# Both final masks of a pair by one minimum and one transposing DMA, in a top-k attention with a highway FFN

## The chip, the cores and the metric

The kernel runs on one core of one Trainium2 chip. Its time is the device time of one execution in microseconds (us); times here are medians of several runs on the same chip. Short names for the engines are those of the profile: PE is TensorE (PEld its weight loads), DVE is VectorE, ACT is ScalarE, POOL is GpSimd, SP is SyncE, whose work here is to issue DMAs.

## The reference

Eight batches of eight heads, 576 rows of 64 per head. Each row of scores keeps only its 32 largest; the others get no weight. The result, heads side by side, goes through a highway layer.

```
scores = scale * q @ k.T                              # 576 x 576 for each head
kth    = the 32nd largest score of each row
scores = where(scores >= kth, scores, -1e9)
attn   = exp(scores - max);  attn = attn / (sum(attn) + 1e-9)
x      = attn @ v, as 4608 x 512
H = relu(x @ w_h);  T = sigmoid(x @ w_t + b_t)
out = T * H + (1 - T) * x
```

## The kernel before, in words

A *unit* is up to 128 query rows of one head against all 576 keys; the last 64 rows of two heads share a unit. There are 288 units, taken two at a time as 144 *pairs*; a batch is 18 pairs. `step(i)` is one turn of a software pipeline over the pairs, and the order of the work on every engine is the order of the calls in `step`: no scheduler moves anything. In step i, pair i is in the middle of its threshold search, pair i+1 begins its own, pair i+2 gets its scores, pair i-1 gets its final mask, and pair i-3 is multiplied with V.

The threshold search of a pair runs as follows. TensorE computes the scores of both units into one tile of PSUM, `xs` (L309, L318; for the tail units L326, L335). VectorE takes the 8 largest of each sixth of a row, twelve instructions a pair (L353, `segments`). `refine` (L366 to L382) merges these into an estimate of the largest value and of a threshold, and writes both to `wall` with the reduction L382. ScalarE then counts with a sign function how many scores lie above the threshold (L397, `mask_count`) and writes a mask that TensorE adds to the scores in PSUM (L410), so that VectorE's next maximum (L420, `below`) finds the largest values below the threshold. From the count and these, L426, L436 (on GpSimd) and L439 pick the exact 32nd largest value. GpSimd multiplies out the biases for the exponential and the mask (L391, `biases`); an explicit dependency makes it wait for the second final mask of the step.

The final mask is made one step later. For the first unit of a pair ScalarE computes `r`, a huge number where the score is at or above the 32nd largest value and zero elsewhere (L443, `above`), and VectorE takes the minimum of the exponentials and `r` (L450, `keep_min`). For the second unit GpSimd computes `ro` as 1 or 0 (L454, `above_one`), and VectorE multiplies (L460, `keep_mul`). In 7 steps GpSimd has too much else, and VectorE makes the second mask in one instruction from the scores (L465, `keep`). Each masked unit goes to its own tile `ep` of 640 columns, 576 and 64 zeros, and SP issues a transposing DMA for each (L481) into a tile `et` of five 128 x 128 blocks. Two steps later TensorE multiplies these with V (L494). V carries a column of ones (L138), so that the sums of the exponentials come out as a 65th column.

Every four heads ScalarE copies the sums out of PSUM (L508, tile `xs` of the pool in SBUF, the same name as the scores' tile). TensorE's filler matmuls (L278, `spare`), which write to a fresh tile of the same PSUM bank, stand behind that copy. When a block of 128 rows has all its heads, its `norm` divides by the sums: VectorE adds 1e-9 and doubles (L557), takes the reciprocal (L559), and GpSimd multiplies in the next step (L564). A GpSimd DMA casts the block to `xb` (L582), SP transposes it to `xT` (L587), and the FFN's matmuls (L522, L532) follow in a later step. The tail of the kernel, `finish`, is written out by hand.

SP issues, in this order in a step: the transposes of the two masks, the transpose of `xb` where one is due, stores, and up to two loads of k and q.

In VectorE's order around the change, one step holds L366, L368, L426, L370, L373, L376, L439, L378, L450, L382, [L557,] L460, [L559,] then L353 of the next pair and L420.

Of the kernel before, what the change touches and what calls it, by code (L numbers as in the profile page):

```python
# [10 lines left out]
ALU = mybir.AluOpType  # L11
# [15 lines left out]
def kernel(  # L27
# [46 lines left out]
    gpool = ctx.enter_context(tc.tile_pool(name="g", bufs=2))  # L74
    epool = ctx.enter_context(tc.tile_pool(name="e", bufs=4))
    cpool = ctx.enter_context(tc.tile_pool(name="c", bufs=4))
    etpool = ctx.enter_context(tc.tile_pool(name="et", bufs=6))
    xpool = ctx.enter_context(tc.tile_pool(name="x", bufs=3))
# [28 lines left out]
    for i in range(NE):  # L107
        en = consts.tile([P, 2, 2, 16], FP32, name=f"en{i}")
        nc.vector.memset(en[:, 0, :, 0:1], 3.0e38)
        ends.append(en)  # L110
    csum = consts.tile([P, NU], FP32)
    nc.vector.memset(wall[:, 0:2, KTH : KTH + 1], 0.0)

    def kth(u):
        return wall[:, u + 2, KTH : KTH + 1]

    def tb(u):
        return be[:, u // 2, u % 2, 0:1]

    def eb(u):  # L120
        return be[:, u // 2 + 1, u % 2, 1:2]
# [14 lines left out]
    for i in range(2):  # L136
        vb = consts.tile([P, H, nck, DE], BF16, name=f"vb{i}")
        nc.gpsimd.memset(vb[:, :, :, D:DE], 1.0)  # L138
        vbs.append(vb)
    NEP = 4  # L140
    eps_sb = []
    for i in range(NEP):
        ep = consts.tile([P, SP], BF16, name=f"ep{i}")
        pad = S if i % 2 == 0 else 0
        nc.vector.memset(ep[:, pad : pad + SP - S], 0.0)
        eps_sb.append(ep)
# [266 lines left out]

    def expo(u, sc):
        e = epool.tile([P, S], BF16, name="e")
        nc.scalar.activation(e[:], sc, AF.Exp, bias=tb(u), scale=scale)  # L416
        return e

    def below(u, ps):
# [14 lines left out]
    def pick_a(pair, hit):  # L434
        u0, u1 = pair[0], pair[1] + 1
        nc.gpsimd.tensor_tensor(hit[:], hit[:], wall[:, u0:u1, THR:KTH], ALU.mult)  # L436
# [3 lines left out]

    def above(u, sc):
        r = epool.tile([P, S], BF16, name="r")
        nc.scalar.activation(r[:], sc, AF.Relu, bias=eb(u), scale=BIGK)  # L443
        return r


    def keep_min(u, e, r):
        ep = eps_sb[u % NEP]
        pad = (u % 2) * (SP - S)
        return ep, nc.vector.tensor_tensor(ep[:, pad : pad + S], e[:], r[:], ALU.min)  # L450

    def above_one(u, sc):
        r = epool.tile([P, S], BF16, name="ro")
        nc.gpsimd.tensor_scalar(r[:], sc, kth(u), None, ALU.is_ge)  # L454
        return r

    def keep_mul(u, e, r):
        ep = eps_sb[u % NEP]
        pad = (u % 2) * (SP - S)
        return ep, nc.vector.tensor_tensor(ep[:, pad : pad + S], e[:], r[:], ALU.mult)  # L460

    def keep(u, sc, e):
        ep = eps_sb[u % NEP]
        pad = (u % 2) * (SP - S)
        return ep, nc.vector.scalar_tensor_tensor(  # L465
            out=ep[:, pad : pad + S],
            in0=sc,
            scalar=kth(u),
            in1=e[:],
            op0=ALU.is_ge,  # L470
            op1=ALU.mult,
        )
# [5 lines left out]

    def transposes(ep):
        et = etpool.tile([P, nck, P], BF16, name="et")  # L480
        nc.sync.dma_start_transpose(et[:], ep[:])  # L481
        return et

# [65 lines left out]
    def ffn_pieces(b, qt, xs):  # L549
# [4 lines left out]
        def norm():  # L554
            xs3 = xs[:, 0 : nh * DE].rearrange("p (h e) -> p h e", e=DE)
            rinv = cpool.tile([P, H], FP32, name="rinv")
            nc.vector.tensor_scalar(rinv[:, 0:nh], xs3[:, :, D], 1e-9, 2.0, ALU.add, ALU.mult)  # L557
            yield
            nc.vector.reciprocal(rinv[:, 0:nh], rinv[:, 0:nh])  # L559
            x = xpool.tile([P, dm], FP32, name="x")  # L560
            st["x"] = x

            def scaled(e):
                e.tensor_tensor(  # L564
                    x[:, 0:w].rearrange("p (h d) -> p h d", h=nh),
                    xs3[:, :, 0:D],
                    rinv[:, 0:nh].unsqueeze(2).to_broadcast([P, nh, D]),
                    ALU.mult,
                )
                if by_dma:  # L570
                    casts.append(cast)
                else:
                    ready.extend([xt, hh, tt])

            pool_work.append((scaled, w))
            yield
# [63 lines left out]
    def blk_norm(k):  # L640
        nh, ng, w = shape_of(k["qt"])
        xs3 = k["xs"][:, 0 : nh * DE].rearrange("p (h e) -> p h e", e=DE)
        k["x"] = xpool.tile([P, dm], FP32, name="x")
        rinv = cpool.tile([P, H], FP32, name="rinv")
        nc.vector.tensor_scalar(rinv[:, 0:nh], xs3[:, :, D], 1e-9, 2.0, ALU.add, ALU.mult)
        nc.vector.reciprocal(rinv[:, 0:nh], rinv[:, 0:nh])
        nc.vector.tensor_tensor(
            k["x"][:, 0:w].rearrange("p (h d) -> p h d", h=nh),
            xs3[:, :, 0:D],
            rinv[:, 0:nh].unsqueeze(2).to_broadcast([P, nh, D]),  # L650
            ALU.mult,
        )
# [122 lines left out]
    def step(i):  # L775
# [25 lines left out]
        if prev:  # L801
            pu, ps_ = pairs[i - 1], st[i - 1]
            ps_["r"] = [above(pu[0], ps_["sc"][0])]
            ps_["r"].append(above_one(pu[1], ps_["sc"][1]) if len(pool_work) < (3 if last_steps else 5) else None)
        if late:
# [6 lines left out]
        ev = prep_filler() if to_prep and (i <= SPB or (len(to_prep) > 15 - k_in or len(layers) > 2) and i % 2) else None  # L812
        do_work(nc.gpsimd, 2 * dm if prev and ps_["r"][1] is None else dm)
        segs(i + 1, 2 * NSEG)
# [3 lines left out]
        if live:  # L818
            st[i]["e"] = [expo(pr[0], st[i]["sc"][0])]
        if nxt:  # L820
# [14 lines left out]
        if live:  # L835
            st[i]["e"].append(expo(pr[1], st[i]["sc"][1]))
            pass
        ra = refine(i + 1, st[i + 1]["cand"]) if nxt else iter(())

        def masked(s):  # L840
            if not prev:
                return None
            u = pu[s]
            if ps_["r"][s] is not None:
                ep, ins = (keep_min, keep_mul)[s](u, ps_["e"][s], ps_["r"][s])
            else:
                ep, ins = keep(u, ps_["sc"][s], ps_["e"][s])
            ps_["et"][s] = transposes(ep)
            return ins
# [3 lines left out]
        if live:  # L853
            hit = hits(pr)
            pick_a(pr, hit)
        added = bool(adds or casts)
        if adds:
# [11 lines left out]
        next(ra, None)  # L869
        masked(0)  # L870
        for _ in ra:
            pass
        scaling = norms.pop(0)() if norms else iter(())
        next(scaling, None)
        last = masked(1)
        if live:
            after(biases(i + 1), last)
        next(scaling, None)
        if nxt:
# [63 lines left out]
    def finish():  # L943
# [29 lines left out]
        while adds:  # L973
            do_add(i)
        relu = above(pu[0], old["sc"][0])
        zh = fps.tile([P, 512], FP32, tag="fp", name="fp")
        ep, last = masked(pu, 1, old)
        old["et"][1] = transposes(ep)
        if pool_work:
# [4 lines left out]
        below(pr[1], cur["ps"][1])  # L984
        es = [expo(u, cur["sc"][s]) for s, u in enumerate(pr)]
        cur["e"] = es
        x1 = xps.tile([P, 3 * BANK], FP32, tag="x", name="xs")
# [4 lines left out]

        hit = hits(pr)
        ep, _ = keep_min(pu[0], old["e"][0], relu)
        old["et"][0] = transposes(ep)
        nc.vector.tensor_tensor(hit[:], hit[:], wall[:, pr[0] : pr[1] + 1, THR:KTH], ALU.mult)
        pick_b(pr, hit)
        x2 = xps.tile([P, 3 * BANK], FP32, tag="x", name="xs")
        cur["et"] = [etpool.tile([P, nck, P], BF16, name="et") for s in range(2)]
        turned = None  # L1000
        for s, home in enumerate((bank(x2, 1), bank(x1, 0))):
            ep, last = masked(pr, s, cur)
            turned = home.bitcast(BF16)[:, 0:SP]
            for c in range(nck):
                nc.tensor.transpose(turned[:, c * P : (c + 1) * P], ep[:, c * P : (c + 1) * P], ident_b[:])
            nc.scalar.copy(cur["et"][s][:].rearrange("p c q -> p (c q)"), turned)
        sure(0, wall[:, 2 : NU + 2, KTH], 1.0)
# [40 lines left out]
    with tc.If(fine < 1):  # L1048
        with tc.For_i(0, B, 1) as bi:
# [26 lines left out]
            for pr in pairs[0 : NG // B]:  # L1076
                scs = copy_scores(scores(pr, prep)[2])
                ets = []
                for s, u in enumerate(pr):
# [13 lines left out]
                    nc.vector.tensor_scalar_mul(tb(u), w[:, 0:1], -scale)  # L1093
                    ep, _ = keep(u, sc, expo(u, sc))
                    ets.append(transposes(ep))
                pso = pso_tile()
# [42 lines left out]
```

## Time and profile before

| | us |
|---|---|
| median of 3 runs | 806.8 (805.77 to 807.28) |
| the profiled execution | 806.17 |
| its span, first to last instruction | 804.5 |
| VectorE busy | 772.8 |
| ScalarE busy | 757.2 |
| TensorE busy | 686.7 |
| GpSimd busy | 559.9 |

All sums below are made against the profiled execution. A row of the timeline has the start, the length, the engine, the line, the operation and its tiles (out<-in), how many instructions it merges, and in brackets how long the engine was idle before it and what ended that wait. A row of the groups has the total busy time and the mean of one in ns, then the idle time before them and its main cause. Rows of SP's queue (SPq) are the issuing of DMAs; the transfer itself lands later.

### The profile page before, as it was taken

How to read it: one execution, taken by the hardware profiler on the slowest of the kernel's cores; microseconds unless marked ns; L12 is line 12 of the kernel's file. 1: busy time of each engine (PE TensorE's matmuls, PEld its weight loads, DVE VectorE, ACT ScalarE, POOL GpSimd, SP SyncE). 2: the span in 40 equal slices, each digit the busy share in tenths (PEclk: the TensorE clock that was granted, in tenths of full speed). 3: DMA queues.
4: the chain of work that ended last, by engine and by line, in shares of the span. 5: the costliest groups of instructions: out<-in, count | busy, mean ns of one | idle time of the engine just before them, and what ended most of it. 6: DMA issues, size and time to landing. Idle time of an engine off the chain costs nothing.

```text
span 804.5 us, 20583 instructions
## 1 busy us (share of the span) xinstructions
PE 686.7 (85%) x6369; PEld 494.7 (61%) x6459; DVE 772.8 (96%) x4020; ACT 757.2 (94%) x1401; POOL 559.9 (70%) x712
## 2 busy tenths in 40 slices
PE   7889998888888888888987889888888888988884
PEld 5666766566666666566665666666666566665662
DVE  5999999999999999999999999999999999999996
ACT  5999999999999999999999999999999999999984
POOL 2666867777777767777767776777776777766750
PEclk9999999999999999999999999999999999999998
DMA  6789968996799667998669766898767996555653
GB/s 121 87 137 159 134 116 140 141 143 93 140 152 148 108 96 137 154 131 125 102 135 159 125 113 107 150 156 126 112 121 136 160 124 109 90 106 110 108 90 88
DMA packets 346359, 100.37 MB, mean 125 GB/s; under 512 B 330624, under 2 KB 338432, under 8 KB 346240
## 3 DMA queue, kind: packets, MB, share of 16 engines
q1 hardware_dynamic: 291024, 79.16, 54.1%
q0 software_dynamic: 53536, 19.34, 22.6%
q8 instruction: 53, 0.87, 0.4%
q10 hardware_dynamic: 1680, 0.46, 0.3%
q14 instruction: 66, 0.54, 0.2%
HBM read 31.72 MB, written 9.44 MB: 51 GB/s over the span
## 4 chain that ended last, share of the span: by engine, by line
ACT 37%; DVE 32%; PE 23%; DMA 4%; issue 3%; SPq 1%; another core or an unknown queue 0%; DVEq 0%; ACTq 0%
ACT m L397 15%; DVE wall L420 12%; DVE cand L353 9%; ACT e L416 7%; ACT sc L348 6%; PE pso L278 5%; ACT r L443 4%; PE xs L309 4%; PE xs L326 3%; DVE ep L450 3%; DMA xT<-xb 3%; PE fp L522 3%; PE xs L410 3%; PE pso L494 2%; ACT xs L508 2%
## 5 line engine op out<-in xcount | busy, mean ns | idle before, releaser
L353 DVE MAX8 cand<-xs 128x8 f32<-128x96 f32 x1728 | 297.5, 248 | 11.4 <-PE xs L335 6.2
L278 PE MATMUL pso<-cst,ident_b 128*128 128x252 bf16 x1841 | 246.8, 272 | 42.8 <-ACT xs L508 40.4
L454 POOL TENSOR_SCALAR ro<-sc,wall 128x576 bf16<-128x576 f32 x135 | 232.8, 1724 | 0.0
L416 ACT ACTIVATE e<-sc,be 128x576 bf16<-128x576 f32 x288 | 226.5, 787 | 0.1
L278 PEld LDWEIGHTS <-ident_b 128*128 128x128 bf16 x1841 | 173.4, 98 | 81.4 <-issue 49.5
L420 DVE MAX8 wall<-xs 128x8 f32<-128x576 f32 x288 | 204.3, 751 | 5.6 <-PE xs L410 3.5
L309 PE MATMUL xs<-kT,qT 64*128 64x256 f32 x1024 | 145.3, 400 | 30.6 <-DVE high L366 26.2
L348 ACT COPY sc<-xs 128x1152 f32<-128x1152 f32 x144 | 161.0, 1118 | 0.7 <-DVE cand L353 0.6
L309 PEld LDWEIGHTS xs<-kT,qT 64*128 64x128 f32 x1024 | 93.0, 186 | 61.3 <-issue 37.6
L397 ACT ACTIVATE m<-xs,wall 128x576 int8<-128x576 f32 x144 | 107.4, 746 | 18.2 <-DVE wall L382 17.1
L436 POOL TENSOR_TENSOR hit<-hit,wall 128x18 f32<-128x18 f32 x143 | 32.4, 227 | 121.2 <-DVE hit L426 114.0
L397 ACT ACTIVATE m<-sc,wall 128x576 int8<-128x576 f32 x144 | 111.4, 773 | 0.0
L443 ACT ACTIVATE r<-sc,be 128x576 bf16<-128x576 f32 x143 | 109.9, 769 | 0.0
L410 PE MATMUL xs<-m,ident_b 128*128 128x512 bf16 (+1 forms) x512 | 92.7, 274 | 17.3 <-ACT m L397 15.2
L494 PEld LDWEIGHTS <-et 128*128 128x128 bf16 (+1 forms) x1600 | 68.6, 100 | 19.2 <-issue 3.5
L391 POOL TENSOR_TENSOR be<-wall,fac 128x4 f32<-128x4 f32 x144 | 29.2, 203 | 72.5 <-DVE ep L460 53.7
L410 PEld LDWEIGHTS <-ident_b 128*128 128x128 bf16 x576 | 51.7, 97 | 44.8 <-issue 24.1
L494 PE MATMUL pso<-vb,et 128*128 128x65 bf16 (+1 forms) x1600 | 74.4, 194 | 4.2 <-DMA et<-ep 0.3
L450 DVE TENSOR_TENSOR ep<-e,r 128x576 bf16<-128x576 bf16 x143 | 64.6, 452 | 0.2 <-ACT r L443 0.2
L318 PEld LDWEIGHTS xs<-kd,qT 128*128 128x128 f32 x256 | 38.1, 188 | 42.5 <-issue 42.1
L318 PE MATMUL xs<-kd,qT 128*128 128x128 f32 x256 | 62.5, 326 | 0.0
L460 DVE TENSOR_TENSOR ep<-e,ro 128x576 bf16<-128x576 bf16 x135 | 60.7, 449 | 0.0
(127 smaller groups left out, 1028.9 us busy)
## 6 DMA issues: line engine op xcount, KB each, us to landing
kin<-in_k_dram SPq DMA_DIRECT2D x64, 128.0 KB, 2.9
qin<-in_q_dram SPq DMA_DIRECT2D x62, 128.0 KB, 3.1
out_dram<-s SPq DMA_DIRECT2D x30, 256.0 KB, 2.8
s<-h POOLq DMA_DIRECT2D x29, 256.0 KB, 4.0
et<-ep SPq DMA_TRANSPOSE x286, 3.3
xb<-x POOLq DMA_DIRECT2D x30, 128.0 KB, 3.0
vb<-in_v_dram POOLq DMA_DIRECT2D x28, 128.0 KB, 4.8
vb<-in_v_dram POOLq DMA_DIRECT2D x24, 64.0 KB, 3.1
```

Of the source, the lines that this page charges most:

```text
L278: nc.tensor.matmul(po["t"][:, 4 * DE : BANK], ident_b[:], cst[:, 0 : BANK - 4 * DE], start=True, stop=True, skip_group_check=True,)
L309: nc.tensor.matmul(ps[:, mo + n0 : mo + n0 + 256], qT[r : r + D, hp, qs : qs + P], kT[r : r + D, hp, n0 : n0 + 256], start=(n0 == 0), stop ...
L318: nc.tensor.matmul(ends, qT[:, hp, qs : qs + P], kd[:, hp, :], start=True, stop=True)
L348: nc.scalar.copy(sc[:], both)
L353: nc.vector.max(cand[:, s, :], sc[:, s * SEG : (s + 1) * SEG])
L397: nc.scalar.activation(m1[:].bitcast(I8)[:, 1 : 2 * S : 2], ps, AF.Sign, bias=wall[:, u, THR : THR + 1], scale=ABOVE, accum_out=csum[:, u ...
L410: nc.tensor.matmul(ps[:, s0:s1], ident_b[:], m1[:, s0:s1], start=False, stop=True, skip_group_check=True)
L416: nc.scalar.activation(e[:], sc, AF.Exp, bias=tb(u), scale=scale)
L420: nc.vector.max(wall[:, u, THR + 1 : KTH], ps)
L443: nc.scalar.activation(r[:], sc, AF.Relu, bias=eb(u), scale=BIGK)
L454: nc.gpsimd.tensor_scalar(r[:], sc, kth(u), None, ALU.is_ge)
L494: nc.tensor.matmul(pso[r0 : r0 + ql, col : col + DE], ets[s][:, c, gi * P2 : gi * P2 + ql], vb[:, h, vc, :], start=(c == 0), stop=(c == nc ...
```

## The change

- `e` and `r` become tiles of a pair (128 x 2 x 576). One minimum, `keep_both`, masks both units; since the exponentials are at most 1, the minimum with GpSimd's 1 or 0 gives the same as the product. Where VectorE makes the second mask from the scores, the two instructions stay.
- `ep` holds both units in 1280 columns, with their 128 zero columns in the middle; one transposing DMA turns it into an `et` of ten blocks.
- The mask is no longer spread through `refine`: it stands behind L382, which so follows L378 directly.
- The column of ones becomes twos, so that the sums come doubled, and the addition of (now) 2e-9 is a GpSimd instruction that reads a constant tile `eps`. It stands right behind L436, and VectorE's reciprocal stands between L378 and L382.
- Buffers: `e` and `r` three pair tiles each (were four single ones for each of e, r and ro), `et` three (were six single), `ep` two (were four single).
- In `finish` the transposes of the last pair but one become one, behind the second mask.

VectorE's order in a step is now L366 to L378 as before, [reciprocal,] L382, the minimum, L353. (Line numbers are those of the kernel before; the changed one has them a few lines later.)

```diff
-        nc.gpsimd.memset(vb[:, :, :, D:DE], 1.0)
+        nc.gpsimd.memset(vb[:, :, :, D:DE], 2.0)
...
-        ep = consts.tile([P, SP], BF16, name=f"ep{i}")
+        ep = consts.tile([P, 2 * SP], BF16, name=f"ep{i}")
...
+    def pair_tile(name):
+        t = epool.tile([P, 2, S], BF16, name=name)
+        return [t[:, s, :] for s in range(2)] + [t]
...
-    def keep_mul(u, e, r):
-        ep = eps_sb[u % NEP]
-        pad = (u % 2) * (SP - S)
-        return ep, nc.vector.tensor_tensor(ep[:, pad : pad + S], e[:], r[:], ALU.mult)
+    def keep_both(u, e, r):
+        ep = eps_sb[u // 2 % NEP]
+        out = bass.AP(tensor=ep.tensor, offset=ep[:].offset, ap=[ep[:].ap[0], [2 * SP - S, 2], [1, S]])
+        return nc.vector.tensor_tensor(out, e[:], r[:], ALU.min)
...
-    def transposes(ep):
-        et = etpool.tile([P, nck, P], BF16, name="et")
-        nc.sync.dma_start_transpose(et[:], ep[:])
-        return et
+    def et_tile():
+        return etpool.tile([P, 2 * nck, P], BF16, name="et")
+    def halves(et):
+        return [et[:, s * nck : (s + 1) * nck, :] for s in range(2)]
+    def transposes(u):
+        et = et_tile()
+        nc.sync.dma_start_transpose(et[:], eps_sb[u // 2 % NEP][:])
+        return halves(et)
...
-            nc.vector.tensor_scalar(rinv[:, 0:nh], xs3[:, :, D], 1e-9, 2.0, ALU.add, ALU.mult)
+            nc.gpsimd.tensor_tensor(rinv[:, 0:nh], xs3[:, :, D], eps[:, 0:nh], ALU.add)
...
-        def masked(s):
+        def masked():
             if not prev:
                 return None
-            u = pu[s]
-            if ps_["r"][s] is not None:
-                ep, ins = (keep_min, keep_mul)[s](u, ps_["e"][s], ps_["r"][s])
+            u, e, r = pu[0], ps_["e"], ps_["r"]
+            if ps_["one"]:
+                ins = keep_both(u, e[2], r[2])
             else:
-                ep, ins = keep(u, ps_["sc"][s], ps_["e"][s])
-            ps_["et"][s] = transposes(ep)
+                keep_min(u, e[0], r[0])
+                ins = keep(u + 1, ps_["sc"][1], e[1])
+            ps_["et"] = transposes(u)
             return ins
...
         if live:
             hit = hits(pr)
             pick_a(pr, hit)
+            scaling = norms.pop(0)() if norms else iter(())
+            next(scaling, None)
...
         if live:
             pick_b(pr, hit)
         next(ra, None)
-        masked(0)
+        if live:
+            next(scaling, None)
         for _ in ra:
             pass
-        scaling = norms.pop(0)() if norms else iter(())
-        next(scaling, None)
-        last = masked(1)
+        last = masked()
         if live:
             after(biases(i + 1), last)
-        next(scaling, None)
...
```

More of the change, by code (lines that the diff above doesn't have):

```diff
@@ L74 @@
     gpool = ctx.enter_context(tc.tile_pool(name="g", bufs=2))
-    epool = ctx.enter_context(tc.tile_pool(name="e", bufs=4))
+    epool = ctx.enter_context(tc.tile_pool(name="e", bufs=3))
     cpool = ctx.enter_context(tc.tile_pool(name="c", bufs=4))
-    etpool = ctx.enter_context(tc.tile_pool(name="et", bufs=6))
+    etpool = ctx.enter_context(tc.tile_pool(name="et", bufs=3))
     xpool = ctx.enter_context(tc.tile_pool(name="x", bufs=3))
@@ L111 @@
     csum = consts.tile([P, NU], FP32)
+    eps = consts.tile([P, H], FP32)
+    nc.vector.memset(eps[:], 2.0e-9)
     nc.vector.memset(wall[:, 0:2, KTH : KTH + 1], 0.0)
@@ L137 @@
         vb = consts.tile([P, H, nck, DE], BF16, name=f"vb{i}")
-        nc.gpsimd.memset(vb[:, :, :, D:DE], 1.0)
+        nc.gpsimd.memset(vb[:, :, :, D:DE], 2.0)
         vbs.append(vb)
-    NEP = 4
+    NEP = 2
     eps_sb = []
     for i in range(NEP):
-        ep = consts.tile([P, SP], BF16, name=f"ep{i}")
-        pad = S if i % 2 == 0 else 0
-        nc.vector.memset(ep[:, pad : pad + SP - S], 0.0)
+        ep = consts.tile([P, 2 * SP], BF16, name=f"ep{i}")
+        nc.vector.memset(ep[:, S : 2 * SP - S], 0.0)
         eps_sb.append(ep)
@@ L412, in mask_add, with expo @@
             )
-    def expo(u, sc):
-        e = epool.tile([P, S], BF16, name="e")
-        nc.scalar.activation(e[:], sc, AF.Exp, bias=tb(u), scale=scale)
-        return e
+    def expo(u, sc, e):
+        nc.scalar.activation(e, sc, AF.Exp, bias=tb(u), scale=scale)
+        return e
+    def pair_tile(name):
+        t = epool.tile([P, 2, S], BF16, name=name)
+        return [t[:, s, :] for s in range(2)] + [t]
     def below(u, ps):
@@ L439, in pick_b, with above, above_one, kept @@
         nc.vector.tensor_reduce(wall[:, pair[0] + 2 : pair[0] + 4, KTH], hit[:], mybir.AxisListType.X, ALU.add)
[L441 to L444, printed above, removed]
-    def keep_min(u, e, r):
-        ep = eps_sb[u % NEP]
-        pad = (u % 2) * (SP - S)
[L450 to L455, printed above, removed]
-    def keep_mul(u, e, r):
-        ep = eps_sb[u % NEP]
-        pad = (u % 2) * (SP - S)
-        return ep, nc.vector.tensor_tensor(ep[:, pad : pad + S], e[:], r[:], ALU.mult)
+    def above(u, sc, r):
+        nc.scalar.activation(r, sc, AF.Relu, bias=eb(u), scale=BIGK)
+    def above_one(u, sc, r):
+        nc.gpsimd.tensor_scalar(r, sc, kth(u), None, ALU.is_ge)
+    def kept(u):
+        o = u % 2 * (2 * SP - S)
+        return eps_sb[u // 2 % NEP][:, o : o + S]
+    def keep_min(u, e, r):
+        return nc.vector.tensor_tensor(kept(u), e, r, ALU.min)
+    def keep_both(u, e, r):
+        ep = eps_sb[u // 2 % NEP]
+        out = bass.AP(tensor=ep.tensor, offset=ep[:].offset, ap=[ep[:].ap[0], [2 * SP - S, 2], [1, S]])
+        return nc.vector.tensor_tensor(out, e[:], r[:], ALU.min)
     def keep(u, sc, e):
[L463 to L466, printed above, removed]
+        return nc.vector.scalar_tensor_tensor(
+            out=kept(u),
             in0=sc,
             scalar=kth(u),
-            in1=e[:],
+            in1=e,
             op0=ALU.is_ge,
@@ L644, in blk_norm @@
         rinv = cpool.tile([P, H], FP32, name="rinv")
-        nc.vector.tensor_scalar(rinv[:, 0:nh], xs3[:, :, D], 1e-9, 2.0, ALU.add, ALU.mult)
+        nc.vector.tensor_tensor(rinv[:, 0:nh], xs3[:, :, D], eps[:, 0:nh], ALU.add)
         nc.vector.reciprocal(rinv[:, 0:nh], rinv[:, 0:nh])
@@ L802, in step @@
             pu, ps_ = pairs[i - 1], st[i - 1]
-            ps_["r"] = [above(pu[0], ps_["sc"][0])]
-            ps_["r"].append(above_one(pu[1], ps_["sc"][1]) if len(pool_work) < (3 if last_steps else 5) else None)
+            ps_["r"] = pair_tile("r")
+            above(pu[0], ps_["sc"][0], ps_["r"][0])
+            ps_["one"] = len(pool_work) < (3 if last_steps else 5)
+            if ps_["one"]:
+                above_one(pu[1], ps_["sc"][1], ps_["r"][1])
         if late:
@@ L812, in step @@
         ev = prep_filler() if to_prep and (i <= SPB or (len(to_prep) > 15 - k_in or len(layers) > 2) and i % 2) else None
-        do_work(nc.gpsimd, 2 * dm if prev and ps_["r"][1] is None else dm)
+        do_work(nc.gpsimd, 2 * dm if prev and not ps_["one"] else dm)
         segs(i + 1, 2 * NSEG)
@@ L818, in step @@
         if live:
-            st[i]["e"] = [expo(pr[0], st[i]["sc"][0])]
+            st[i]["e"] = pair_tile("e")
+            expo(pr[0], st[i]["sc"][0], st[i]["e"][0])
         if nxt:
@@ L835, in step @@
         if live:
-            st[i]["e"].append(expo(pr[1], st[i]["sc"][1]))
-            pass
+            expo(pr[1], st[i]["sc"][1], st[i]["e"][1])
         ra = refine(i + 1, st[i + 1]["cand"]) if nxt else iter(())
-        def masked(s):
+        def masked():
             if not prev:
                 return None
-            u = pu[s]
-            if ps_["r"][s] is not None:
-                ep, ins = (keep_min, keep_mul)[s](u, ps_["e"][s], ps_["r"][s])
-            else:
-                ep, ins = keep(u, ps_["sc"][s], ps_["e"][s])
-            ps_["et"][s] = transposes(ep)
+            u, e, r = pu[0], ps_["e"], ps_["r"]
+            if ps_["one"]:
+                ins = keep_both(u, e[2], r[2])
+            else:
+                keep_min(u, e[0], r[0])
+                ins = keep(u + 1, ps_["sc"][1], e[1])
+            ps_["et"] = transposes(u)
             return ins
@@ L974, in finish @@
             do_add(i)
-        relu = above(pu[0], old["sc"][0])
+        r = pair_tile("r")
+        above(pu[0], old["sc"][0], r[0])
         zh = fps.tile([P, 512], FP32, tag="fp", name="fp")
-        ep, last = masked(pu, 1, old)
-        old["et"][1] = transposes(ep)
+        last = masked(pu, 1, old)
         if pool_work:
@@ L984, in finish @@
         below(pr[1], cur["ps"][1])
-        es = [expo(u, cur["sc"][s]) for s, u in enumerate(pr)]
-        cur["e"] = es
+        cur["e"] = pair_tile("e")
+        for s, u in enumerate(pr):
+            expo(u, cur["sc"][s], cur["e"][s])
         x1 = xps.tile([P, 3 * BANK], FP32, tag="x", name="xs")
@@ L993, in finish @@
         hit = hits(pr)
-        ep, _ = keep_min(pu[0], old["e"][0], relu)
-        old["et"][0] = transposes(ep)
+        keep_min(pu[0], old["e"][0], r[0])
+        old["et"] = transposes(pu[0])
         nc.vector.tensor_tensor(hit[:], hit[:], wall[:, pr[0] : pr[1] + 1, THR:KTH], ALU.mult)
@@ L998, in finish @@
         x2 = xps.tile([P, 3 * BANK], FP32, tag="x", name="xs")
-        cur["et"] = [etpool.tile([P, nck, P], BF16, name="et") for s in range(2)]
+        cur["et"] = halves(et_tile())
         turned = None
         for s, home in enumerate((bank(x2, 1), bank(x1, 0))):
-            ep, last = masked(pr, s, cur)
+            masked(pr, s, cur)
+            ep = eps_sb[pr[0] // 2 % NEP][:, s * SP : (s + 1) * SP]
             turned = home.bitcast(BF16)[:, 0:SP]
@@ L1005, in finish @@
                 nc.tensor.transpose(turned[:, c * P : (c + 1) * P], ep[:, c * P : (c + 1) * P], ident_b[:])
-            nc.scalar.copy(cur["et"][s][:].rearrange("p c q -> p (c q)"), turned)
+            nc.scalar.copy(cur["et"][s].rearrange("p c q -> p (c q)"), turned)
         sure(0, wall[:, 2 : NU + 2, KTH], 1.0)
@@ L1077 @@
                 scs = copy_scores(scores(pr, prep)[2])
-                ets = []
                 for s, u in enumerate(pr):
@@ L1093 @@
                     nc.vector.tensor_scalar_mul(tb(u), w[:, 0:1], -scale)
-                    ep, _ = keep(u, sc, expo(u, sc))
-                    ets.append(transposes(ep))
+                    e = pair_tile("e")[s]
+                    keep(u, sc, expo(u, sc, e))
+                ets = transposes(pr[0])
                 pso = pso_tile()
```

## The prediction

> **What bounds the kernel now.** I read the page's engine totals first, then the chain that ended last, then the costliest groups with what ended their idle time.
>
> ```profile
> PE 686.7 (85%) x6369; PEld 494.7 (61%) x6459; DVE 772.8 (96%) x4020; ACT 757.2 (94%) x1401; POOL 559.9 (70%) x712
> ...
> ACT 37%; DVE 32%; PE 23%; DMA 4%; issue 3%; SPq 1%; another core or an unknown queue 0%; DVEq 0%; ACTq 0%
> ...
> L397 ACT ACTIVATE m<-xs,wall 128x576 int8<-128x576 f32 x144 | 107.4, 746 | 18.2 <-DVE wall L382 17.1
> ```
>
> VectorE is busy 96% and ScalarE 94%, yet the chain gives ScalarE the larger share and TensorE a quarter: three engines take turns. The last row matters most: ScalarE idles 17.1 us waiting for L382, the maximum that gives the next pair's threshold, and the change moves L382. So I went to the timeline, first to VectorE's rows in one plain step (from one L366 to the next):
>
> ```profile
> 354.98 0.19 DVE L366 TENSOR_TENSOR high<-cand 128x48 f32<-128x48 f32 x1
> ...
> 355.85 0.19 DVE L378 SCALAR_TENSOR_TENSOR cand<-en 128x16 f32<-128x16 f32 x1
> 355.94 0.45 DVE L450 TENSOR_TENSOR ep<-e,r 128x576 bf16<-128x576 bf16 x1
> 356.31 0.21 DVE L382 TENSOR_REDUCE wall<-cand 128x4 f32<-128x32 f32 x1
> 356.43 0.45 DVE L460 TENSOR_TENSOR ep<-e,ro 128x576 bf16<-128x576 bf16 x1
> 356.80 2.08 DVE L353 MAX8 cand<-xs 128x8 f32<-128x96 f32 x12
> 358.79 1.41 DVE L420 MAX8 wall<-xs 128x8 f32<-128x576 f32 x2
> 360.12 0.19 DVE L366 TENSOR_TENSOR high<-cand 128x48 f32<-128x48 f32 x1
> ```
>
> A row's length includes a tail under which the next instruction already starts (L450 is 0.45 long, L382 starts after 0.37), so I price by the distance between starts. The step takes 5.14 us with no gap, so here VectorE alone sets the pace; from L366 to L353 it needs 1.82. Two other engines stand close behind, as another step shows:
>
> ```profile
> 301.33 0.19 DVE L366 TENSOR_TENSOR high<-cand 128x48 f32<-128x48 f32 x1
> ...
> 302.62 0.49 PE L318 MATMUL xs<-kd,qT 128*128 128x128 f32 x2
> 302.66 0.20 DVE L382 TENSOR_REDUCE wall<-cand 128x4 f32<-128x32 f32 x1
> ...
> 302.90 0.74 ACT L397 ACTIVATE m<-xs,wall 128x576 int8<-128x576 f32 x1
> ```
>
> The scores that L353 reads are done 1.78 after L366 (303.11), 0.04 before VectorE would want them: a tie. ScalarE starts L397 0.04 after L382's end: it was waiting. And where a block of sums is copied out, TensorE's filler waits for that copy and the scores come late:
>
> ```profile
> 338.75 1.02 PE L278 MATMUL pso<-cst,ident_b 128*128 128x252 bf16 x8 [0.98 <-ACT xs L508]
> ...
> 338.97 0.19 DVE L366 TENSOR_TENSOR high<-cand 128x48 f32<-128x48 f32 x1
> ...
> 341.29 2.07 DVE L353 MAX8 cand<-xs 128x8 f32<-128x96 f32 x12 [0.23 <-PE xs L318]
> ```
>
> There L353 comes 2.32 after L366 instead of 1.82. The copy is ScalarE's, a few instructions behind L397.
>
> **The change part by part.**
>
> *One minimum instead of two.* From L378 to L353 now (rows above): 0.09 to L450, 0.37 to L382, 0.12 to L460, 0.37 to L353, 0.95 in all. L450 covers the time for which L382 must wait for L378. Without that cover the trace shows the pair at the start:
>
> ```profile
> 13.33 0.19 DVE L378 SCALAR_TENSOR_TENSOR cand<-en 128x16 f32<-128x16 f32 x1
> 13.55 0.21 DVE L382 TENSOR_REDUCE wall<-cand 128x4 f32<-128x32 f32 x1
> ```
>
> 0.22. The merged minimum is in no trace. L353 takes 1.99/12 = 0.166 for 96 columns and L420 1.33/2 = 0.665 for 576, so a fixed 0.065 and one column in 1.04 ns. L450's 0.37 for 576 is then 0.07 fixed and 0.30 at two columns in that time; 1152 columns take 0.67. Bounds: 0.37 below (one old half), 0.74 above (both in full). I take 0.67, since L353 and L420 show the fixed part to be paid once an instruction. After: 0.22 + 0.12 + 0.67 = 1.01. **So a plain step gets 0.06 us longer on VectorE**, though two instructions became one.
>
> *L382 earlier.* It starts 0.22 behind L378, not 0.46: ScalarE's mask count may start 0.24 earlier. How much of it ScalarE can use is bounded by 0 (it is busy 94%) and 0.24; the 17.1 us of waits are 0.12 over 144 steps, and somewhat more between starts, as rows carry a tail. I take 0.15. Late next are the sums' copy, the filler and the scores behind it, which move forward with ScalarE.
>
> *The sums' constant.* In 38 steps VectorE's addition goes to GpSimd:
>
> ```profile
> 307.43 0.19 DVE L378 SCALAR_TENSOR_TENSOR cand<-en 128x16 f32<-128x16 f32 x1
> ...
> 308.57 0.38 DVE L353 MAX8 cand<-xs 128x8 f32<-128x96 f32 x2
> ...
> L436 POOL TENSOR_TENSOR hit<-hit,wall x143: 224/227/232, 17.8 to 780.8; 128x18 f32<-128x18 f32 x143
> ```
>
> Now 1.14 from L378 to L353; after, the reciprocal sits in the uncovered 0.22, so 1.01: 0.13 less. GpSimd's addition is priced like L436 just ahead of it, 0.23. L436 starts some 0.47 after L366, the addition so ends near 0.93, and the reciprocal is due at 0.96: hidden by a hair, else it holds L382, the minimum and the transposes. Queued behind it on GpSimd are that step's DMA issue and the bias product, which waits for the minimum anyhow. What hides the addition is VectorE's refinement; uncovered it would cost 0.23 a time.
>
> *One transposing DMA a pair.* SP issues two a pair now, then the FFN's:
>
> ```profile
> L481 SPq DMA_TRANSPOSE et<-ep x286: 1199/1223/2522, 23.9 to 786.1; - x143
> L587 SPq DMA_TRANSPOSE xT<-xb x37: 1168/1217/2357, 69.6 to 767.7; - x37
> PEld L522 <- DMA xT<-xb: 6.7, 10, 1.6
> ```
>
> An issue costs 1.22 for five blocks of 128 columns and 1.22 for the FFN's four or two: it is fixed, so ten blocks are put at 1.25 (bounds 1.22 and 2.44). The issue starts about 0.55 later, because it waits for the merged mask, but one issue is gone: what follows on SP (xT, the loads of k and q, the stores) starts 0.7 earlier, or 0.5 later at the upper bound. TensorE waits for xT, ten times and up to 1.6; eight steps pass 0.23 or more of it on to L420. I take xT 0.5 earlier. The masks are used two steps on, so 1 us there is hidden, except at the end.
>
> *The end.* The last pair but one had one of its transposes issued early; now both go together:
>
> ```profile
> 788.78 0.83 PE L494 MATMUL pso<-vb,et 128*64 128x65 bf16 x20 [0.27 <-DMA et<-ep]
> ```
>
> It is already waited for. Twice the data: 0 to 1.2 more (a whole issue), taken 0.8. The buffers hold as many pairs as before or enough for the pair two steps back; the memsets are set-up; both are put at nothing.
>
> *Sum.* I cut VectorE's timeline at L366 into 141 whole steps and shifted each by what bounds it there:
>
> - 56 plain steps like the one shown (mean 5.17): 0.06 less small waits, +2.6.
> - 18 that wait for TensorE ahead of L420 by about 0.1 (mean 5.25): the wait absorbs it, 0.
> - 38 with late scores (mean 5.46): 0.15 earlier, until VectorE's own 1.88 bounds them, -4.7.
> - 5 more with the sums' constant: -0.6.
> - 16 whose scores are the tail tile's (mean 5.82): TensorE decides, -0.2.
> - 8 with a late xT (mean 5.84): -3.5.
> - The end: +0.8.
>
> In all -5.6. The profiled execution took 806.2 (span 804.5, 1.7 around it), which makes 800.6; the median of the runs lies 0.6 above it, so I say **801**.
>
> **Rivals**, from the median 806.8.
>
> *No help.* ScalarE and TensorE may hold the late steps by their own work, not through L382, and xT may wait for its data, not for SP. Then VectorE's own sum is left: 56 plain steps +2.6, norm steps with room (late ones too) -1.6, the end +0.8: +1.8, 808.6. For it: ScalarE is 94% busy. Against it: L397 starts right at L382's end.
>
> *Slower: the uncovered wait.* If the merged minimum costs 0.74 and no head start arrives, plain steps pay 0.13; the same recount gives +6.1 and the end +0.8: 813.7. With the head start kept, 0.74 gives +1.2; the turn lies at 0.72.
>
> *Slower: GpSimd holds VectorE.* The trace shows one holding the other:
>
> ```profile
> 283.76 1.27 POOL L610 TENSOR_TENSOR s<-h,x 128x512 f32<-128x512 f32 x1 [0.81 <-ACT h L609]
> ...
> 284.44 0.66 DVE L366 TENSOR_TENSOR high<-cand 128x48 f32<-128x48 f32 x1
> ```
>
> L366 takes 0.66 instead of 0.19 and ends 0.07 after L610. The new addition runs just ahead of L378, which like L366 reads two tiles, and of the reciprocal that needs it. Held for its whole 0.23 in all 38 steps: +8.7, so -5.6 becomes +3.1, 809.9; from 0.15 a step on it decides. Against it: by the starts above they overlap by 0.03 or so. The Trainium skill, page "SBUF — State Buffer", section "Who interferes with whom", has a VectorE instruction with two SBUF inputs contend with a GpSimd one that reads SBUF, and the first to start blocks the other; by that rule L378 too would wait in these steps, and the L366 row agrees with it.
>
> *Stronger.* With the full 0.24 and 0.76 the recount gives -7.9, with the end -7.1; with a minimum of 0.43 on top, -13.7: 793 to 800.
>
> *One column in 1.04 ns* for the merged minimum, whose output has a gap: 0.6 more in 135 steps, +81. No row speaks for it.
>
> **How the numbers follow.** Forecast (796 to 805) 0.54; stronger 0.07; no help 0.15; uncovered wait 0.11; GpSimd 0.11; slow minimum 0.02. A measurement of this kernel can tell about 0.2% from no change; no help lies on that edge and is halved. Faster 0.61, same 0.08, slower 0.31. The range reaches to the GpSimd case and the stronger one, and leaves out the uncovered wait at its worst: 795.5 to 812.
>
> **What would show it.** Right: a merged row near 0.75 long and 0.67 to L353; L382 0.22 behind L378; ScalarE's wait for L382 well under 17.1; L353 in copying steps nearer 1.9 after L366; 143 transposes of masks at 1.25; the wait for xT well under 6.7. Wrong: a merged row over 0.82; L378 over 0.19 or a reciprocal that waits for GpSimd; late steps as late as before; xT landing no earlier; a new wait of TensorE for the masks.

## The result, and the profile after

The changed kernel took 803.0 us (median of 5 runs, 802.7 to 803.5) against 806.8 for the kernel before: a ratio of 0.9954, with an interval of 0.9942 to 0.9965. It is faster by about half a per cent. The profiled execution took 803.5, its span is 801.9.

The page of the changed kernel: busy times, the chain that ended last, ScalarE's first mask count, and the new minimum.

```profile
PE 685.3 (85%) x6369; PEld 494.0 (62%) x6459; DVE 768.5 (96%) x3846; ACT 759.3 (95%) x1401; POOL 564.9 (70%) x750
...
DVE 65%; ACT 15%; PE 12%; DMA 3%; issue 3%; SPq 1%; DVEq 0%; ACTq 0%
...
L398 ACT ACTIVATE m<-xs,wall 128x576 int8<-128x576 f32 x144 | 108.0, 750 | 11.0 <-DVE wall L383 9.4
...
L463 DVE TENSOR_TENSOR ep<-e,r 128x1152 bf16<-128x1152 bf16 x135 | 100.9, 748 | 0.4 <-ACT e L416 0.4
```

VectorE's share of the chain has gone from 32% to 65%: ScalarE's wait for the threshold's reduction (now L383) has fallen from 17.1 to 9.4 us, and VectorE sets the pace in most steps. The timeline of VectorE shows the same plain step as before, and then one with a reciprocal, with GpSimd's new addition ahead of it:

```profile
354.32 0.19 DVE L367 TENSOR_TENSOR high<-cand 128x48 f32<-128x48 f32 x1
...
355.19 0.19 DVE L379 SCALAR_TENSOR_TENSOR cand<-en 128x16 f32<-128x16 f32 x1
355.41 0.21 DVE L383 TENSOR_REDUCE wall<-cand 128x4 f32<-128x32 f32 x1
355.54 0.75 DVE L463 TENSOR_TENSOR ep<-e,r 128x1152 bf16<-128x1152 bf16 x1
356.20 2.06 DVE L354 MAX8 cand<-xs 128x8 f32<-128x96 f32 x12
```

```profile
306.57 0.20 POOL L564 TENSOR_TENSOR rinv<-xs,eps 128x8 f32<-128x8 f32 x1
...
306.79 0.19 DVE L379 SCALAR_TENSOR_TENSOR cand<-en 128x16 f32<-128x16 f32 x1
306.88 0.20 DVE L566 RECIPROCAL rinv<-rinv 128x8 f32<-128x8 f32 x1
307.01 0.21 DVE L383 TENSOR_REDUCE wall<-cand 128x4 f32<-128x32 f32 x1
307.14 0.75 DVE L463 TENSOR_TENSOR ep<-e,r 128x1152 bf16<-128x1152 bf16 x1
307.80 2.06 DVE L354 MAX8 cand<-xs 128x8 f32<-128x96 f32 x12
```

From L379 to L354 both take 1.01. The reduction starts 0.22 behind L379 in either; the reciprocal sits in that gap and waits for nothing. GpSimd's addition ends just before L379 starts. Next, a step in which the sums are copied out:

```profile
338.08 1.02 PE L279 MATMUL pso<-cst,ident_b 128*128 128x252 bf16 x8 [0.98 <-ACT xs L515]
...
338.59 0.19 DVE L367 TENSOR_TENSOR high<-cand 128x48 f32<-128x48 f32 x1
...
340.62 2.07 DVE L354 MAX8 cand<-xs 128x8 f32<-128x96 f32 x12
```

It is the step shown before at 338.97. L354 now stands 2.03 behind L367 instead of 2.32: still late, but less. Last, SP's transposes, in the groups by line and the waits, then SP's rows of one step and TensorE's behind it:

```profile
L488 SPq DMA_TRANSPOSE et<-ep x143: 1253/1387/2433, 24.2 to 783.3; - x143
...
L594 SPq DMA_TRANSPOSE xT<-xb x37: 1167/1327/1743, 68.6 to 764.1; - x37
...
DMA to landing us min/median/max: 2.4/3.1/4.6
...
PEld L529 <- DMA xT<-xb: 6.2, 9, 1.3
...
399.29 1.38 SPq L488 DMA_TRANSPOSE et<-ep  x1
400.75 1.33 SPq L594 DMA_TRANSPOSE xT<-xb  x1
...
405.65 0.81 PE L529 MATMUL fp<-wh,xT 128*128 128x512 bf16 x3 [1.33 <-DMA xT<-xb]
```

An issue of ten blocks takes 1.39 (median), but TensorE waits for xT nearly as it did: 6.2 us against 6.7 before.

To see where the time went I cut VectorE's timeline of every kernel at L366 (L367) and put each step into the class that the prediction gave it. The numbers are us against the profiled execution of the kernel before, summed over the class; the last two rows are the span and the ratio of the medians.

| class (steps) | predicted | changed | e1 | e2 | e3 | e4 | e5 | e6 | e7 | e8 | e9 | e10 |
|---|---|---|---|---|---|---|---|---|---|---|---|---|
| plain (56) | +2.6 | +4.1 | +4.8 | +13.2 | +4.7 | +7.5 | +1.2 | +4.8 | +1.2 | +7.8 | +4.8 | 0.0 |
| waits at L420 (18) | 0 | +0.1 | +0.5 | +2.4 | +0.1 | +0.9 | -0.3 | -0.3 | -0.6 | +0.6 | -0.2 | 0.0 |
| late scores (38) | -4.7 | -4.9 | -3.5 | +3.2 | -3.7 | -1.1 | -4.4 | -4.7 | -4.9 | -3.0 | -4.8 | -0.1 |
| other norm (5) | -0.6 | -0.2 | +0.1 | +0.8 | 0.0 | +0.7 | -0.4 | -0.4 | -0.4 | 0.0 | -0.4 | 0.0 |
| tail tile (16) | -0.2 | -0.1 | 0.0 | +0.2 | 0.0 | 0.0 | +0.3 | 0.0 | +0.3 | 0.0 | 0.0 | 0.0 |
| late xT (8) | -3.5 | -1.6 | +4.1 | -2.3 | -2.0 | +2.1 | -1.9 | -5.1 | -5.1 | +1.2 | -4.5 | -4.6 |
| span | 804.5 | 801.9 | 810.6 | 822.9 | 803.3 | 814.1 | 798.8 | 798.2 | 794.9 | 810.8 | 799.4 | 799.2 |
| ratio | | 0.9954 | 1.0130 | 1.0209 | 0.9977 | 1.0104 | 0.9901 | 0.9897 | 0.9859 | 1.0026 | 0.9939 | 0.9925 |

(Under "predicted" the span is that of before. What the classes leave over is mostly the start, where the first L366 comes 0.3 to 1.0 earlier in the other kernels than in that one execution; nothing in the change explains that, and it isn't counted as a gain.)

### The profile page after: what moved, and what is told of

It is laid out like the page before. It is cut to its first block, busy times and chain, and to the rows that moved or that the text cites. A ratio compares the mean times of both kernels' runs of the same rounds, so it can differ in the third digit from the quotient of the medians.

```text
span 801.9 us, 20159 instructions
## 1 busy us (share of the span) xinstructions
PE 685.3 (85%) x6369; PEld 494.0 (62%) x6459; DVE 768.5 (96%) x3846; ACT 759.3 (95%) x1401; POOL 564.9 (70%) x750
## 4 chain that ended last, share of the span: by engine, by line
DVE 65%; ACT 15%; PE 12%; DMA 3%; issue 3%; SPq 1%; DVEq 0%; ACTq 0%
DVE cand L354 24%; DVE wall L424 19%; DVE ep L463 8%; ACT m L398 5%; PE xs L327 4%; ACT e L416 3%; ACT sc L349 3%; DMA xT<-xb 2%; DVE en L374 2%; DVE en L377 2%; DVE cand L379 2%; PE fp L529 2%; ACT r L446 2%; DVE high L367 2%; PE pso L279 2%
## 5 line engine op out<-in xcount | busy, mean ns | idle before, releaser
L354 DVE MAX8 cand<-xs 128x8 f32<-128x96 f32 x1728 | 297.0, 247 | 9.7 <-PE xs L336 6.5
L449 POOL TENSOR_SCALAR r<-sc,wall 128x576 bf16<-128x576 f32 x135 | 232.5, 1722 | 0.0
L424 DVE MAX8 wall<-xs 128x8 f32<-128x576 f32 x288 | 203.9, 749 | 5.1 <-PE xs L411 2.5
L463 DVE TENSOR_TENSOR ep<-e,r 128x1152 bf16<-128x1152 bf16 x135 | 100.9, 748 | 0.4 <-ACT e L416 0.4
L411 PE MATMUL xs<-m,ident_b 128*128 128x512 bf16 (+1 forms) x512 | 90.6, 274 | 9.1 <-ACT m L398 7.0
L618 POOL TENSOR_TENSOR h<-h,x 128x512 f32<-128x512 f32 (+1 forms) x37 | 43.0, 1161 | 0.6
```

What stands on the lines that cost most here:

```text
L354: nc.vector.max(cand[:, s, :], sc[:, s * SEG : (s + 1) * SEG])
L411: nc.tensor.matmul(ps[:, s0:s1], ident_b[:], m1[:, s0:s1], start=False, stop=True, skip_group_check=True)
L424: nc.vector.max(wall[:, u, THR + 1 : KTH], ps)
L449: nc.gpsimd.tensor_scalar(r, sc, kth(u), None, ALU.is_ge)
L463: return nc.vector.tensor_tensor(out, e[:], r[:], ALU.min)
```

## The experiments

The runs came in three groups, on different chips. Each was timed beside the kernel before, and its ratio is to that kernel's time there: 808.1 us beside e1 to e4, 807.9 beside e5 to e8, 807.2 beside e9 and e10.

My theory after the result was: the gain is ScalarE's and TensorE's head start in the late steps; it pays for a longer plain step; the one DMA gives nothing. The first four runs test this.

**e1, two transposing DMAs again.**

```diff
 def transposes(u):
     et = et_tile()
-    nc.sync.dma_start_transpose(et[:], eps_sb[u // 2 % NEP][:])
+    for s, half in enumerate(halves(et)):
+        nc.sync.dma_start_transpose(half, eps_sb[u // 2 % NEP][:, s * SP : (s + 1) * SP])
     return halves(et)
```

> The changed kernel, but with two transposing DMAs a pair again, both issued behind the merged minimum. Theory 'threshold' (the gain comes from L382's earlier start; the merged DMA gives nothing, since the FFN's transpose is held by the masks' data ahead of it): 802.5 to 804.5, and TensorE's wait for xT stays near 6 us although xT is issued about 1.2 us later. Rival 'queue' (one issue less on SP is what pays): 805 or more, with a longer wait for xT.

Measured: ratio 1.013 (1.0105 to 1.0156), 817.9 us. My theory fell here. The profiled execution is the fastest of its runs (812.3, the others 814.5 to 821.6), so its trace shows only the lower part of the loss. In the five longer runs the granted clock of TensorE was also lower, 0.988 to 0.995 against 0.996, so how much of the rest is due to the two DMAs is open. The table puts the part in the trace on the late xT: +5.7 against the changed kernel in eight steps. The waits of e1, and SP's rows for the step shown above (the second of the two mask transposes, then xT):

```profile
PEld L530 <- DMA xT<-xb: 14.7, 15, 2.2
...
DVE wall L424 <- PE xs L411: 9.5, 11, 2.0
...
402.91 1.27 SPq L489 DMA_TRANSPOSE et<-ep  x1
404.27 1.22 SPq L595 DMA_TRANSPOSE xT<-xb  x1
```

TensorE waits for xT fifteen times instead of nine. Counted from L366 (L367), xT is issued 4.2 us on (median) before, 3.5 in the changed kernel, 4.7 here. So with the masks in their later place the one DMA matters: with two, xT is issued later than before the change, with one earlier. What one DMA would be worth with the masks in their old place no run here shows.

**e2, the mask ahead of the reduction.**

```diff
-        if live:
-            next(scaling, None)
-        for _ in ra:
-            pass
         last = masked()
+        if live:
+            next(scaling, None)
+        for _ in ra:
+            pass
```

> The changed kernel, but the merged minimum stands ahead of the threshold's reduction again, so that it covers the reduction's wait. VectorE's own path from L379 to L354 then falls from 1.01 to 0.88 us, and the reduction starts 0.76 instead of 0.22 behind L379. Theory 'threshold': slower than the kernel before, 811 or more, because ScalarE's count starts 0.3 later than there and the late steps grow. Rival 'vector' (what counts is VectorE's own work): faster than the changed kernel, 803 - 56 x 0.13 = 796.

Measured: ratio 1.0209 (1.0194 to 1.0224), 824.6 us: 'threshold', clearly. The timeline and the page of e2:

```profile
363.72 0.19 DVE L379 SCALAR_TENSOR_TENSOR cand<-en 128x16 f32<-128x16 f32 x1
363.81 0.75 DVE L463 TENSOR_TENSOR ep<-e,r 128x1152 bf16<-128x1152 bf16 x1
364.48 0.21 DVE L383 TENSOR_REDUCE wall<-cand 128x4 f32<-128x32 f32 x1
364.66 1.58 DVE L354 MAX8 cand<-xs 128x8 f32<-128x96 f32 x9
...
ACT 41%; DVE 32%; PE 21%; issue 3%; DMA 2%; SPq 1%; DVEq 0%; ACTq 0%
...
L398 ACT ACTIVATE m<-xs,wall 128x576 int8<-128x576 f32 x144 | 107.2, 744 | 34.8 <-DVE wall L383 32.8
```

VectorE reaches L354 0.94 behind L379, earlier than in the changed kernel, and gives it back: ScalarE waits 32.8 us for the reduction, and VectorE then waits at L424. Against the kernel before, the loss is in the plain steps (+13.2) more than in the late ones (+3.2), which I had not expected.

**e3, the sums' constant on VectorE.**

```diff
-            nc.gpsimd.tensor_tensor(rinv[:, 0:nh], xs3[:, :, D], eps[:, 0:nh], ALU.add)
+            nc.vector.tensor_tensor(rinv[:, 0:nh], xs3[:, :, D], eps[:, 0:nh], ALU.add)
```

> The changed kernel, but the addition of the sums' constant is VectorE's, at the place where GpSimd has it. VectorE gets 0.07 to 0.09 us longer in 38 steps, of which many wait for the scores anyway. Theory 'threshold': 803.5 to 806, a small loss. Rival 'GpSimd' (the addition on GpSimd holds L379 or the reciprocal up): 803 or less.

Measured: ratio 0.9977 (0.9966 to 0.9987), 805.9 us. As expected: the addition on GpSimd is worth 0.2%. Nor does it hold anything up in the changed kernel: L379 takes 0.19 in all 144 steps there.

**e4, the kernel before with the reduction first.**

```diff
-        masked(0)
         for _ in ra:
             pass
+        masked(0)
```

> The kernel before, but with both of its masks behind the reduction L382: the reordering alone, without the merged minimum, the one DMA and GpSimd's addition. From L378 to L353 it takes 0.22 + 0.12 + 0.37 + 0.37 = 1.08 instead of 0.95. Theory 'threshold': the late steps gain nearly what they gain in the changed kernel (-3 to -5 in all), the plain ones lose 0.13 each (+6 to +8): 808 to 811. Rival 'vector': the 0.13 is paid in nearly every step, +18: 820 or more. Rival 'head start alone': 802, as in the changed kernel.

Measured: ratio 1.0104 (1.0088 to 1.012), 815.8 us against 808.1 beside it. It lies between the theories, above the range of mine. Plain steps lose 7.5 as expected; the late steps gain only 1.1, since VectorE's own path, now 1.08 behind L378 and more where a norm stands in it, becomes their bound: its idle time ahead of L353 falls from 11.4 to 6.0 us, so in part of the steps it is now VectorE that is late, and no longer the scores. And xT costs 2.1 more, as it costs more in e1. The reordering by itself is a loss.

**e8, two minimums.** The merging alone, undone.

```diff
-                ins = keep_both(u, e[2], r[2])
+                keep_min(u, e[0], r[0])
+                ins = keep_min(u + 1, e[1], r[1])
```

> The changed kernel, with two minimums of one unit each instead of the merged one, both behind the threshold's reduction, and one DMA. Measures the merging alone. Each has a fixed part of about 0.07: VectorE's path from L379 to L354 is 1.08 instead of 1.01 in 135 steps. Theory: +0.07 in plain steps and part of it in the late ones, +4 to +7, ratio 1.000 to 1.004. Rival 'the DMA is all that counts': ratio 0.995 to 0.997.

Measured: ratio 1.0026 (1.0013 to 1.004), 810.5 us, in the range of the theory. One fixed part of 0.07 us in 135 steps is worth about 0.7%. The profiled execution was the slowest of its twelve (812.5), and in its trace one late-xT step alone is 2.7 longer than in the changed kernel; without it that class would stand at -1.5 in the table, not at +1.2.

The next runs take up the two losses that the trace of the changed kernel shows.

**e5, the gap filled.** In steps without a reciprocal the minimum is cut at column 64 of each unit.

```diff
+        if split:
+            keep_both(pu[0], ps_["e"][2], ps_["r"][2], 0, CUT)      # CUT = 64
         for _ in ra:
             pass
         last = masked()                                           # then columns CUT to S
```

> The changed kernel, but in steps without a reciprocal the merged minimum is cut in two: 64 columns of both units (128 elements, about 0.13 us) stand between L379 and the threshold's reduction and cover its wait, the other 512 columns of both follow it. From L379 to L354 it should take 0.09 + 0.13 + 0.13 + 0.60 = 0.95 instead of 1.01, with the reduction still 0.22 behind L379. Theory 'uncovered wait' (a plain step is longer by what the reduction waits): 60 to 75 steps gain 0.055, -3 to -4, so a ratio to the kernel before of 0.990 to 0.992 against 0.9954 of the changed kernel. Rival 'scores decide': same as the changed kernel, since the scores arrive just as VectorE is free.

Measured: ratio 0.9901 (0.9877 to 0.9925), 800.4 us. The timeline of the plain step:

```profile
353.54 0.19 DVE L379 SCALAR_TENSOR_TENSOR cand<-en 128x16 f32<-128x16 f32 x1
353.63 0.22 DVE L465 TENSOR_TENSOR ep<-e,r 128x128 bf16<-128x128 bf16 x1
353.76 0.21 DVE L383 TENSOR_REDUCE wall<-cand 128x4 f32<-128x32 f32 x1
353.88 0.68 DVE L465 TENSOR_TENSOR ep<-e,r 128x1024 bf16<-128x1024 bf16 x1
354.48 2.07 DVE L354 MAX8 cand<-xs 128x8 f32<-128x96 f32 x12
```

0.94 to L354, with the reduction at 0.22. The plain steps get back 2.9 of their 4.1 us: the uncovered wait was most of their loss.

**e6, xT first.**

```diff
+        while turns and turns[0][0] <= i and len(flying) < 2:
+            turns.pop(0)[1]()
         last = masked()
...
-        while turns and turns[0][0] <= i and len(flying) < 2:
-            turns.pop(0)[1]()
```

> The changed kernel, but where the FFN's transpose is due SP issues it ahead of the masks' transpose. Theory 'data' (xT is issued earlier in the changed kernel but lands no earlier, because ten blocks of masks go through ahead of it): TensorE's wait for xT falls from 6 us to 2 or less, and the time by 1.5 to 3.5, ratio 0.991 to 0.9935. Rival 'landing' (the transfer itself is slow in these steps, whatever is ahead of it): wait and time as in the changed kernel, 0.995.

Measured: ratio 0.9897 (0.987 to 0.9925), 800.0 us. This is more than expected. No wait of TensorE for the transfer of xT is left in the list of waits, and the late-xT steps give 5.1 instead of 1.6. SP's rows in that step, and the time from issue to landing of xT, in e6 and then in e10 below:

```profile
396.42 1.24 SPq L594 DMA_TRANSPOSE xT<-xb  x1
397.76 1.35 SPq L488 DMA_TRANSPOSE et<-ep  x1
...
DMA to landing us min/median/max: 2.3/3.0/6.1
...
DMA to landing us min/median/max: 2.4/3.4/5.6
```

'Landing' forecast no change, and that is out. But its idea is not refuted, and 'data' is not shown: xT takes a median of 3.0 us from issue to landing here, as long as in the changed kernel (3.1), though the step's own masks no longer stand ahead of it; in e10 it takes 3.4 against 2.6 in the kernel before. What removes the wait is the earlier issue. Once xT need not stand behind the masks, SP mostly issues it as the step before ends, 3.9 us earlier than in the changed kernel (median of the 37). Why the landing takes 3.1 in the changed kernel, against 2.6 before and 2.5 in e1, stays open.

**e7, both.** The edits of e5 and e6 together.

> Both of the above. If the two losses are separate, the gains add up: ratio 0.986 to 0.990. If both only wait for the same third thing, it is as the better of the two.

Measured: ratio 0.9859 (0.9832 to 0.9887), 796.9 us. The gains add up within the intervals (the two ratios together would give 0.984), and this version beats both kernels.

**e9, two DMAs and xT first.** The edits of e1 and e6 together.

> The changed kernel with two transposing DMAs a pair and the FFN's transpose ahead of them. Theory 'xT alone' (the second issue costs only through the FFN's transpose behind it): the loss of the two DMAs goes, ratio 0.989 to 0.992, as with one DMA and xT first (0.9897). Rival 'SP is full' (the second issue also holds loads, stores or the masks themselves up): 0.996 or more.

Measured: ratio 0.9939 (0.9925 to 0.9953), 802.2 us. Between the two: most of e1's loss goes, so it was xT's. Some 0.4% stays against e6. In the traces the two differ by 1.1 us, of which 0.5 is one step that still waits for xT and 0.3 is the start; the rest isn't settled, and the two ran on different chips.

**e10, the kernel before with xT first.** The same loop over `turns`, moved ahead of `masked(0)` in the kernel before.

> The kernel before with nothing changed but SP's order: the FFN's transpose ahead of the step's two mask transposes. Its eight steps with a late xT lose their wait at L420, 4.5 us in all in the profile of before: theory 'data' 803.5 to 805, ratio 0.994 to 0.997. Rival 'landing': no change, 0.999 to 1.001.

Measured: ratio 0.9925 (0.9912 to 0.9939), 801.1 us, a little more than expected. The table shows that only the late-xT steps move. This one reordering of SP's queue gives more than the whole change.

## Why the prediction was right

The direction holds, and the time lies in the range: 801 was forecast, 803.0 measured, within 795.5 to 812. Between the medians 3.8 us came. But the sum of 5.6 was made against the profiled execution, and between the two profiled executions only 2.7 came (806.2 to 803.5); the other 1.1 is how these two lie to the medians of their kernels. The steps below account for the 2.7. The mechanism was right, an earlier L382 against a longer plain step, but two terms were too hopeful, the plain steps by 1.5 and the transposing DMA by 1.9. By its steps:

- *One minimum*: taken at 0.67 from start to start, measured 0.67 (median; 355.54 to 356.20 in the step shown). The "one column in 1.04 ns" rival and the 0.74 are out. The reduction uncovered starts 0.22 behind L379, as taken from the only pair at the start of the trace. e8 shows what the merging itself is worth.
- *Plain steps*: +2.6 was said, +4.1 came. In 46 of the 56 the loss is 0.05 each, as worked out (+2.2 in all); ten lose 0.12 to 0.36 (+1.9), which the sum had not. In two of these, the worst with 0.36 each, the merged minimum waits for ScalarE's exponentials, as it now needs both units at once. In five a VectorE instruction overlaps one of GpSimd and takes longer, the rival's mechanism, but at L367 and with another instruction. One step of each kind:

```profile
87.70 0.76 DVE L463 TENSOR_TENSOR ep<-e,r 128x1152 bf16<-128x1152 bf16 x1 [0.22 <-ACT e L416]
...
374.63 0.73 POOL L618 TENSOR_TENSOR h<-h,x 128x256 f32<-128x256 f32 x1
...
375.09 0.33 DVE L367 TENSOR_TENSOR high<-cand 128x48 f32<-128x48 f32 x1
```

L367 takes 0.33 and not 0.19, and ends 0.06 after L618. Over the kernel such longer rows cost 0.5 us more than before.
- *Late steps*: -4.7 was said with a head start of 0.15, -4.9 came. e2 turns it round (+3.2), so L382's place is the cause, and e4 and e8 show that a head start is worth only what VectorE's own path leaves of it. That the size fits so well is partly luck: in these steps ScalarE's count starts about 0.2 earlier, not 0.15, but L354 only about 0.1. Of the 4.9, e3 takes back 1.2, which is GpSimd's addition.
- *The sums' constant*: hidden by a hair, it was said; the reciprocal starts 0.09 behind L379 in all 38 steps. The addition took 0.20 and not 0.23, and ended 0.10 before the reciprocal started and just before L379 did. So the two never overlapped at L379, and what an overlap there would cost was not tested. e3 gives the addition 0.2%. The five other steps with it gained 0.2 in all, not 0.6: four gain a little under 0.1 each, and one loses 0.14.
- *One transposing DMA*: this step failed. "I take xT 0.5 earlier" was worth -3.5, and -1.6 came. SP does issue xT 0.7 earlier (median of the 37 transposes), but the transfer takes longer from issue to landing (3.1 against 2.6). In the eight steps of this class xT is issued 0.84 earlier on average and lands only 0.25 earlier, and the steps get 0.20 shorter each, where the sum had 0.44. TensorE's wait stays at 6.2, partly because two other steps now wait. So the half of the "no help" rival that said "xT may wait for its data, not for SP" is right in that the landing took back most of the earlier issue; why it took longer is open (e6). The issue of ten blocks took 1.39, not 1.25.
- *The end*: 0 to 1.2 more, taken 0.8. TensorE's wait there grew, but from the last L367 on the kernel is only 0.2 longer:

```profile
786.67 0.83 PE L501 MATMUL pso<-vb,et 128*64 128x65 bf16 x20 [1.03 <-DMA et<-ep]
```

## What to carry to other kernels

When three engines take turns, ask of a reordering who is released earlier and not only how much work is saved: here VectorE's path got longer and the kernel got faster. And e2 and e5 have nearly the same path (0.94 from L379 to L354), yet e2 was the slowest of all and e5 faster than the changed kernel: in e2 the reduction that ScalarE waits for stands 0.76 behind L379, in e5 0.22. An instruction that has to wait for the one just before it leaves a gap; fill it with a piece cut to that length (e5) and not with the whole work, which would delay what others wait for. And look at the order within a DMA queue before merging transfers: putting the one that is waited for first (e10) gave more here than the whole change.

## What was not expected of the hardware

The issue of a transposing DMA is nearly the same for ten blocks as for five: 1.39 us (median) against 1.22. Masks issued as two halves and late cost up to 1.8% of the kernel, mostly through one transfer behind them (e1 against the changed kernel, e9 against e6); e1's runs also spread over 9 us, where those of the other variants stay within 3.5. Its longer runs have the lower granted clocks; why, the traces don't show. And a VectorE instruction with two inputs, L367, got longer next to one of GpSimd in four plain steps where it had not before, though the change moved neither in its engine's order; its row is longer and shows no wait ahead of it.
